# One kernel in two stages becomes one stream of 128-token units, with the attention output kept on chip

## The chip, the cores and the metric

The kernel runs on one core of one Trainium2 chip. A core has a matrix engine (PE, whose weight loads are shown as PEld), a vector engine (DVE), an activation engine (ACT), a general engine (POOL), and a queue engine (SP) that issues transfers. Fast memory (SBUF) has 128 partitions; PE writes into accumulation banks (PSUM). The metric is the device time of one execution in microseconds (us). The time of a kernel is the median of several runs.

## The reference

The inputs q, k and v have 8 batches, 8 heads, 576 tokens and 64 elements per head. Each token attends to the tokens at most 32 places away:

```
scores = (q @ k^T) / 8          where |i - j| <= 32, else masked
attn   = exp(scores) / row sum  (a maximum is subtracted first, which cancels)
a      = attn @ v
x      = a, heads side by side: 4608 tokens x 512
h      = x @ w_in               512 x 2048
g      = h * sigmoid(1.702 h)
out    = g @ w_out              2048 x 512, float32
```

All inputs are float32. The kernels compute the products in bfloat16.

## The kernel before, in words

It runs in two stages, one behind the other, with the attention output in device memory between them (`x_bridge`).

**Attention** goes over 8 batches. For q and k it loads five blocks of 128 tokens (the last has 64), 256 KB each in runs of 256 bytes (L81), casts each to bfloat16 on DVE (L83), transposes four pairs of heads on PE (L86) and copies the result out of PSUM on DVE (L87). Then it goes over nine blocks of 64 queries. For each it loads its window of 128 keys of v again (L94, nine loads of 256 KB a batch), casts it on ACT (L96), multiplies eight heads' scores (L104, 64x64), takes the exponential in two halves into float32 (L107), casts these to bfloat16 (L109), cuts the band with two selects on POOL (L110, L113), multiplies with v and a column of ones (L120), and divides by the sum (L125, L127). The 64 rows of x go to device memory (L128).

**The two layers (MLP)** begin with the weights: 4 loads of w_in (L147) and 16 of w_out (L152), each with a DVE cast (L148, L153). Then nine tiles of 512 tokens follow. Each loads x transposed, by four transposing transfers (L159). In 16 steps `ff`, four matmuls of 512 columns make one 128-row piece of h (L165), ACT makes g from it (L168), and four matmuls add it into four banks of output (L170). Four copies (L174) and four stores (L175) close the tile; `o_sb` has two buffers, and the four output banks have one each.

A planner orders the instructions of each engine. Transfers all go through SP's queue, in order; the MLP's pools open when those of attention have closed.

## Time and profile before

| what | value |
|---|---|
| runs shown | 595.07, 594.59, 594.83 us; median 594.83 |
| the profiled execution | its own time is given as its span, 594.3 us; the runs' median is 0.5 us above it |
| busy, share of the span | PE 64%, PEld 31%, DVE 29%, ACT 36%, POOL 17% |
| transfers | 65.51 MB in 183333 packets, 171520 of them under 512 bytes |
| device memory | read 46.14 MB, written 14.16 MB |

A share of busy time is a mean over stages that differ. PE's matmuls are pipelined: their shown durations overlap, so a row's whole length over its count is the pace, and the mean of one is its latency. "Idle before" says how long an engine waited ahead of a group and what ended that wait. The granted clock is the share of PE's full clock of 2.4 GHz.

### The profile page before, as it was taken

Reading aid. Unit: us, or ns where it says so; the run is one execution under the profiler, and the core shown is the slowest. Engines: PE = TensorE matmul, PEld = TensorE weight load, DVE = VectorE, ACT = ScalarE, POOL = GpSimd, SP = SyncE. Lnnn points to the kernel's source line nnn. Section 1 sums busy time; section 2 is a strip of 40 time slices with the busy share of each in tenths; the row PEclk is TensorE's granted clock in tenths of the full one; section 3 lists DMA queues with packets and bytes.
Section 4 is the critical chain, followed back from the end, with each engine's and each line's share of the span. In section 5 each row is a group of like instructions: output and inputs, shape, how many; then the busy total and the mean of one; then the engine's idle time right before and its main releaser. Section 6 shows DMA issues by size and latency. Waiting matters only on the chain.

```text
span 594.3 us, 7458 instructions
## 1 busy us (share of the span) xinstructions
PE 379.6 (64%) x2624; PEld 186.8 (31%) x2624; DVE 170.9 (29%) x504; ACT 213.6 (36%) x434; POOL 102.0 (17%) x222
## 2 busy tenths in 40 slices
PE   2525335252533525253069798997989898989994
PEld 1423223141322414232024343333334333333431
DVE  2545445454543535454222200000010101010101
ACT  1725436172543617246013233232323232323331
POOL 0613416071341606235000000000000000000000
PEclk9999999999999999999999999899989999999999
DMA  7576685857668576765865302102030303030101
GB/s 166 122 167 147 156 183 129 184 126 156 144 156 185 128 168 140 152 145 121 296 149 174 111 16 67 41 19 88 10 98 1 106 1 106 1 103 4 72 0 72
DMA packets 183333, 65.51 MB, mean 110 GB/s; under 512 B 171520, under 2 KB 176128, under 8 KB 182784
## 3 DMA queue, kind: packets, MB, share of 16 engines
q1 hardware_dynamic: 183296, 65.03, 44.4%
q8 instruction: 21, 0.34, 0.3%
q14 instruction: 16, 0.13, 0.1%
HBM read 46.14 MB, written 14.16 MB: 101 GB/s over the span
## 4 chain that ended last, share of the span: by engine, by line
PE 39%; SPq 5%; DMA 5%; issue 2%; DVE 2%; ACT 0%; DVEq 0%; ACTq 0%
PE ops L170 20%; PE h_ps L165 19%; SPq L159 5%; DMA out_dram<-o_sb 3%; DVE o_sb L174 1%; DMA wtmp<-in_moe_w_in_dram 1%; DMA xT<-x_bridge 1%; DVE w_in_sb L148 0%; ACT g_sb L168 0%; DVEq L174 0%; SPq L152 0%; SPq L175 0%; DVEq L148 0%; ACTq L168 0%
## 5 line engine op out<-in xcount | busy, mean ns | idle before, releaser
L168 ACT ACTIVATE g_sb<-h_ps 128x512 bf16<-128x512 f32 x144 | 85.9, 597 | 218.1 <-PE h_ps L165 218.1
L165 PE MATMUL h_ps<-xT,w_in_sb 128*128 128x512 bf16 x576 | 146.4, 391 | 22.1 <-DVE w_out_sb L153 18.9
L170 PE MATMUL ops<-w_out_sb,g_sb 128*128 128x512 bf16 x576 | 144.1, 384 | 21.9 <-DVE o_sb L174 20.8
L86 PE MATMUL tps<-ident,qktmp 128*128 128x128 bf16 (+1 forms) x320 | 45.1, 293 | 86.2 <-DVE qktmp L83 82.0
L174 DVE COPY o_sb<-ops 128x512 f32<-128x512 f32 x36 | 23.8, 689 | 237.9 <-PE ops L170 198.8
L120 PE MATMUL oa<-v_aug,pbf 128*64 128x65 bf16 x576 | 47.4, 245 | 63.2 <-ACT v_aug L96 53.1
L165 PEld LDWEIGHTS <-w_in_sb 128*128 128x128 bf16 x576 | 57.5, 100 | 95.3 <-issue 31.6
L96 ACT CAST v_aug<-v_f 128x512 bf16<-128x512 f32 x72 | 44.6, 620 | 107.1 <-DMA v_f<-in_v_dram 104.2
L170 PEld LDWEIGHTS <-g_sb 128*128 128x128 bf16 x576 | 46.3, 98 | 108.0 <-ACT g_sb L168 46.8
L110 POOL TENSOR_SCALAR_AFFINE_SELECT pbf<-pbf 128x512 bf16<-128x512 bf16 x72 | 47.8, 663 | 157.8 <-ACT pbf L109 157.8
L107 ACT ACTIVATE p<-sc 128x256 f32<-128x256 f32 x144 | 49.1, 389 | 35.6 <-PE sc L104 35.2
L120 PEld LDWEIGHTS <-pbf 128*64 128x64 bf16 x576 | 38.3, 153 | 72.8 <-issue 42.1
L86 PEld LDWEIGHTS <-qktmp 128*128 128x128 bf16 (+1 forms) x320 | 26.0, 128 | 100.0 <-DVE qktmp L83 97.9
L127 DVE TENSOR_TENSOR ob<-oa,inv 64x256 bf16<-64x256 f32 x144 | 56.1, 410 | 1.2 <-DVE inv L125 0.5
L113 POOL TENSOR_SCALAR_AFFINE_SELECT pbf<-pbf 128x512 bf16<-128x512 bf16 x72 | 49.7, 690 | 2.8
L109 ACT CAST pbf<-p 128x512 bf16<-128x512 f32 x72 | 44.8, 622 | 9.5 <-PE oa L120 7.6
L83 DVE CAST qktmp<-qktmpf 128x512 bf16<-128x512 f32 (+1 forms) x80 | 37.5, 469 | 34.3 <-DMA qktmpf<-in_q_dram 22.4
L125 DVE RECIPROCAL inv<-oa 64x4 f32<-64x4 f32 x144 | 19.2, 162 | 70.5 <-PE oa L120 70.2
L104 PE MATMUL sc<-qT,kT 64*128 64x64 bf16 x576 | 28.8, 236 | 14.6 <-DVE kT L87 8.1
L104 PEld LDWEIGHTS <-kT 64*128 64x128 bf16 x576 | 18.8, 120 | 24.2 <-DVE kT L87 16.6
L87 DVE COPY qT<-tps 128x512 bf16<-128x512 bf16 (+1 forms) x40 | 15.9, 397 | 24.2 <-PE tps L86 24.2
L87 DVE COPY kT<-tps 128x512 bf16<-128x512 bf16 (+1 forms) x40 | 15.8, 395 | 15.4 <-PE tps L86 15.4
(11 smaller groups left out, 23.2 us busy)
## 6 DMA issues: line engine op xcount, KB each, us to landing
v_f<-in_v_dram SPq DMA_DIRECT2D x72, 256.0 KB, 3.5
out_dram<-o_sb SPq DMA_DIRECT2D x36, 256.0 KB, 2.1
qktmpf<-in_q_dram SPq DMA_DIRECT2D x32, 256.0 KB, 3.5
qktmpf<-in_k_dram SPq DMA_DIRECT2D x32, 256.0 KB, 3.3
x_bridge<-ob SPq DMA_DIRECT2D x72, 64.0 KB, 2.1
wtmp<-in_moe_w_in_dram SPq DMA_DIRECT2D x4, 1024.0 KB, 5.3
wtmp<-in_moe_w_out_dram SPq DMA_DIRECT2D x16, 256.0 KB, 2.6
qktmpf<-in_q_dram SPq DMA_DIRECT2D x8, 128.0 KB, 3.0
```

The source lines that it names most:

```text
L86: nc.tensor.transpose(tps[:, hp, :si], tmp[:si, hp * 2:hp * 2 + 2, :], ident[:si, :si])
L96: nc.scalar.copy(vt[:, :, :D], vtf)
L104: nc.tensor.matmul(scl[eo][:, hq, :], kT[hr:hr + D, hp, ks0:ks0 + 128], qT[hr:hr + D, hp, q0:q0 + SQ], start=(hq == 0), stop=(hq == 3))
L107: nc.scalar.activation(pbig[:, eo, :, :], scl[eo], AF.Exp, scale=scale)
L109: nc.scalar.copy(pbf, pbig)
L110: nc.gpsimd.affine_select(out=pbf, in_=pbf, compare_op=ALU.is_ge, fill=0.0, base=off + 32, pattern=[[0, 2], [0, 4], [-1, SQ]], channel_mul ...
L113: nc.gpsimd.affine_select(out=pbf, in_=pbf, compare_op=ALU.is_ge, fill=0.0, base=-off + 32, pattern=[[0, 2], [0, 4], [1, SQ]], channel_mul ...
L120: nc.tensor.matmul(oal[eo][:, hq, :], pbf[:, eo, hq, :], vt[:, h, :], start=(hq == 0), stop=(hq == 3))
L127: nc.vector.tensor_mul(obig[:, :, eo, :], oal[eo][:, :, :D], inv_b)
L165: nc.tensor.matmul(h_ps, w_in_sb[:, kr, ff * 128:(ff + 1) * 128], xT[:, kr, :], start=(kr == 0), stop=(kr == NK - 1))
L168: nc.scalar.activation(g_sb, h_ps, AF.Gelu_apprx_sigmoid)
L170: nc.tensor.matmul(o_ps[ts], g_sb[:, ts * 128:(ts + 1) * 128], w_out_sb[:, ff, :], start=(ff == 0), stop=(ff == NFF - 1))
```

## The change

The two stages become one program of 36 units of 128 tokens (two query blocks each) and nine tiles of 512 tokens (four units), written out by hand in the order that each engine keeps (`manual_schedule`). `head` runs the first tile apart; from unit 8 on `run` puts into one step: scores of unit n, the second layer of tile t-2, transposes of a coming batch, values of unit n, and the first layer of tile t-1.

x is transposed on PE from SBUF (`x_T`) and never leaves the chip. q and k are loaded with six neighbouring tokens per partition (96 partitions, runs of 1536 bytes). v is loaded once, into key blocks of 128 that begin at even windows (`ve`); the odd windows (`vo`) are copied from there by transfers between partitions on POOL's queue. The exponential is written in bfloat16, and the band is cut by a DVE product with a mask that is made once. The second layer runs over the whole g of a tile, one 128-row block of output at a time.

```diff
+    def bank(self, kind, shape, dtype, name):
+        bufs = {"h": 2, "o": 1, "sc0": 1, "sc1": 1, "pv0": 1, "pv1": 1, "tp": 1}[kind]
+        return self.ps.tile(shape, dtype, name=name, tag=kind, bufs=bufs)
+
...
+        self.w_out_sb = cst.tile([128, self.NFF, self.DM], BF16, name="w_out_sb")
+        self.qT = [cst.tile([128, 4, self.S], BF16, name=f"qT{i}") for i in range(2)]
+        self.kT = [cst.tile([128, 4, self.S + 64], BF16, name=f"kT{i}") for i in range(2)]
+        self.ve = [cst.tile([128, 5, self.H, 66], BF16, name=f"ve{i}") for i in range(2)]
...
+    def setup_mask(self):
+        m = self.mask
+        self.nc.gpsimd.memset(m, 1.0)
+        for i in range(5):
+            blk = m[:, i * SQ:(i + 1) * SQ]
+            _select(self.nc, blk, 0, -1, 1)
+            _select(self.nc, blk, 64, 1, -1)
+            if i == 2:
+                _select(self.nc, blk, 95, 0, -1)
+            if i == 3:
+                _select(self.nc, blk, -32, 0, 1)
+
...
+    def load_w_in(self, c):
+        w = self.DFF // 4
+        raw = self.raw.tile([128, self.NK, w], F32, name="w_raw", tag="w_raw", bufs=2)
+        self.nc.sync.dma_start(raw, self.w_in[:, c * w:(c + 1) * w].rearrange("(k p) f -> p k f", p=128))
+        self.raws["wi", c] = raw
+
+    def cast_w_in(self, c, eng):
+        w = self.DFF // 4
+        raw = self.raws.pop(("wi", c))
+        for kr in range(self.NK):
+            self.cast(eng, self.w_in_sb[:, kr, c * w:(c + 1) * w], raw[:, kr, :])
+
+    def load_w_out(self, c):
+        raw = self.raw.tile([128, 4, self.DM], F32, name="w_raw", tag="w_raw", bufs=2)
+        self.nc.sync.dma_start(raw, self.w_out[512 * c:512 * (c + 1), :].rearrange("(k p) f -> p k f", p=128))
+        self.raws["wo", c] = raw
+
+    def cast_w_out(self, c, eng):
+        raw = self.raws.pop(("wo", c))
+        for fr in range(4):
+            self.cast(eng, self.w_out_sb[:, 4 * c + fr, :], raw[:, fr, :])
+
+    def load_qk(self, b, parts=1):
+        for name, src in (("k", self.k), ("q", self.q)):
+            self.raws[name, b] = self.raw.tile([PT, self.H, JT * self.D], F32, name=name + "_raw", tag=name + "_raw")
+        n = self.H // parts
+        for i in range(parts):
+            for name, src in (("k", self.k), ("q", self.q)):
+                self.nc.sync.dma_start(self.raws[name, b][:, i * n:(i + 1) * n, :],
+                                       src[b, i * n:(i + 1) * n].rearrange("h (p j) d -> p h (j d)", j=JT))
+
+    def cast_qk(self, b, which, hp, eng):
+        keep = self.ks if which == "k" else self.qs
+        if hp == 0:
+            keep[b] = self.work.tile([PT, 4, JT, 2, self.D], BF16, name=which + "s", tag=which + "s")
+        raw = self.raws[which, b][:, 2 * hp:2 * hp + 2, :].rearrange("p h (j d) -> p j h d", d=self.D)
+        self.cast(eng, keep[b][:, hp], raw)
+
+    def load_v(self, b):
+        raw = self.raw.tile([128, 5, self.H, self.D], F32, name="v_raw", tag="v_raw")
+        for m in range(5):
+            lo, hi, p = self.v_rows(m)
+            self.nc.sync.dma_start(raw[p, m, :, :], self.v[b, :, lo:hi, :].rearrange("h s d -> s h d"))
+        self.raws["v", b] = raw
+
+    def v_rows(self, m):
+        lo, hi = max(0, 128 * m - 32), min(self.S, 128 * m + 96)
+        p0 = lo - (128 * m - 32)
+        return lo, hi, slice(p0, p0 + hi - lo)
+
+    def cast_v(self, b, m, eng):
+        p = self.v_rows(m)[2]
+        for s in ([slice(32, 64), slice(64, 128)] if p.start else [p]):
+            self.cast(eng, self.ve[b % 2][s, m, :, :self.D], self.raws["v", b][s, m, :, :])
+
+    def shift_v(self, b, lo, hi):
+        ve, vo = self.ve[b % 2], self.vo[b % 2]
+        self.nc.gpsimd.dma_start(vo[0:64, lo:hi, :, :], ve[64:128, lo:hi, :, :])
+        self.nc.gpsimd.dma_start(vo[64:128, lo:hi, :, :], ve[0:64, lo + 1:hi + 1, :, :])
+
+    def heads_T(self, b, which, hp, kind="tp", eng=None):
+        nc = self.nc
+        src = (self.ks if which == "k" else self.qs)[b]
+        tp = self.bank(kind, [128, JT, PT], BF16, "tp")
+        for j in range(JT):
+            nc.tensor.transpose(tp[:, j, :], src[:, hp, j],
+                                self.ident[:PT, :PT])
+        if which == "k":
+            dst = self.kT[b % 2][:, hp, 32:32 + self.S]
+        else:
+            dst = self.qT[b % 2][:, hp, :]
+        self.cast(eng or nc.vector, dst.rearrange("r (p j) -> r p j", j=JT), tp.rearrange("r j p -> r p j"))
+
+    def blocks(self, u):
+        return [divmod(2 * u + i, NB) for i in range(2)]
+
+    def scores(self, u):
+        nc = self.nc
+        sc = [self.bank(f"sc{eo}", [128, 4, 2, SQ], F32, f"sc{eo}") for eo in range(2)]
+        n = 0
+        for blk, (b, j) in enumerate(self.blocks(u)):
+            for hp in range(4):
+                for eo in range(2):
+                    r = slice(eo * 64, eo * 64 + 64)
+                    nc.tensor.matmul(sc[eo][:, hp, blk, :], self.kT[b % 2][r, hp, 64 * j:64 * j + 128],
+                                     self.qT[b % 2][r, hp, 64 * j:64 * j + 64],
+                                     start=(n == 0), stop=(n == 7))
+                n += 1
+        p = self.work.tile([128, 2, 4, 2, SQ], BF16, name="p", tag="p", bufs=5)
+        for eo in range(2):
+            nc.scalar.activation(p[:, eo], sc[eo], AF.Exp, scale=self.scale)
+        self.p[u] = p
+
+    def band(self, u):
+        nc = self.nc
+        p = self.p[u]
+        (b0, j0), (b1, j1) = self.blocks(u)
+        first = {8: 2, 7: 1}.get(j0, 3 if j0 == 0 else 0)
+        msk = self.mask[:, first * SQ:(first + 2) * SQ].rearrange("p (o w) -> p o w", o=1)
+        for eo in range(2):
+            pv = p[:, eo].rearrange("p h b s -> p h (b s)")
+            nc.vector.tensor_mul(pv, pv, msk.to_broadcast([128, 4, 2 * SQ]))
+
+    def values(self, u):
+        nc, D = self.nc, self.D
+        p = self.p.pop(u)
+        x = self.work.tile([128, self.H, D], BF16, name="x", tag="x", bufs=3)
+        rec = self.work.tile([128, self.H, 1], F32, name="rec", tag="rec", bufs=3)
+        acc = [self.bank(f"pv{i}", [128, 4, D + 1], F32, f"pv{i}") for i in range(2)]
+        for half in range(2):
+            for hh in range(4):
+                h = 4 * half + hh
+                for blk, (b, j) in enumerate(self.blocks(u)):
+                    vt = (self.vo if j % 2 else self.ve)[b % 2]
+                    nc.tensor.matmul(acc[half][blk * 64:blk * 64 + 64, hh, :], p[:, h % 2, h // 2, blk, :],
+                                     vt[:, j // 2, h, :D + 1], start=(hh == 0), stop=(hh == 3))
+        for half in range(2):
+            hs = slice(4 * half, 4 * half + 4)
+            nc.vector.reciprocal(rec[:, hs, :], acc[half][:, :, D:D + 1])
+            nc.vector.tensor_mul(x[:, hs, :], acc[half][:, :, :D], rec[:, hs, :].to_broadcast([128, 4, D]))
+        self.x[u] = x
+
+    def x_T(self, u):
+        nc = self.nc
+        t, s = divmod(u, 4)
+        if s == 0:
+            self.xT[t] = self.work.tile([128, self.NK, 512], BF16, name="xT", tag="xT")
+        x = self.x.pop(u)
+        tp = self.bank("tp", [128, 4, 128], BF16, "tp")
+        for c in range(4):
+            nc.tensor.transpose(tp[:, c, :], x[:, 2 * c:2 * c + 2, :], self.ident)
+        nc.vector.tensor_copy(self.xT[t][:, :, s * 128:(s + 1) * 128], tp)
+
+    def layer1(self, t, ff):
+        nc = self.nc
+        if ff == 0:
+            self.g[t] = self.work.tile([128, self.NFF, 512], BF16, name="g", tag="g")
+        hps = self.bank("h", [128, 512], F32, "h_ps")
+        for kr in range(self.NK):
+            nc.tensor.matmul(hps, self.w_in_sb[:, kr, ff * 128:(ff + 1) * 128], self.xT[t][:, kr, :],
+                             start=(kr == 0), stop=(kr == self.NK - 1))
+        nc.scalar.activation(self.g[t][:, ff, :], hps, AF.Gelu_apprx_sigmoid)
+
+    def layer2(self, t, s, quarter, kind="o"):
+        nc = self.nc
+        if quarter == 0:
+            self.o_ps[t, s] = self.bank(kind, [128, self.DM], F32, "o_ps")
+        o_ps = self.o_ps[t, s]
+        for ff in range(4 * quarter, 4 * quarter + 4):
+            nc.tensor.matmul(o_ps, self.g[t][:, ff, s * 128:(s + 1) * 128], self.w_out_sb[:, ff, :],
+                             start=(ff == 0), stop=(ff == self.NFF - 1))
+        if quarter == 3:
+            o_sb = self.work.tile([128, self.DM], F32, name="o_sb", tag="o_sb", bufs=4)
+            nc.vector.tensor_copy(o_sb, o_ps)
+            row = t * 512 + s * 128
+            nc.sync.dma_start(self.out[row:row + 128, :], o_sb)
+
+    def head(self):
+
+        nc, dve, act = self.nc, self.nc.vector, self.nc.scalar
+        self.load_qk(0, parts=4)
+        self.setup()
+        self.load_v(0)
+        for c in range(2):
+            self.load_w_in(c)
+        kinds = ("h", "tp", "h", "o")
+        for hp in range(4):
+            self.cast_qk(0, "k", hp, dve)
+            self.cast_qk(0, "q", hp, act)
+            self.heads_T(0, "k", hp, kinds[(2 * hp) % 4], dve)
+            self.heads_T(0, "q", hp, kinds[(2 * hp + 1) % 4], act)
+        self.setup_mask()
+        for u in range(4):
+            self.scores(u)
+            self.cast_v(0, u, dve)
+            if u > 0:
+                self.shift_v(0, u - 1, u)
+            self.band(u)
+        self.cast_v(0, 4, dve)
+        self.shift_v(0, 3, 4)
+        self.load_w_in(2)
+        self.load_w_in(3)
+        self.load_qk(1, parts=4)
+        self.cast_w_in(0, act)
+        for u in range(4):
+            self.values(u)
+            self.x_T(u)
+        for c in range(2):
+            self.load_w_out(c)
+        for ff in range(16):
+            if ff in (0, 4, 8):
+                self.cast_w_in(ff // 4 + 1, dve)
+            self.layer1(0, ff)
+            if ff >= 9 and ff % 2:
+                hp = (ff - 9) // 2
+                self.cast_qk(1, "k", hp, dve)
+                self.cast_qk(1, "q", hp, dve)
+                self.heads_T(1, "k", hp)
+                self.heads_T(1, "q", hp, "o")
+        self.load_w_out(2)
+        self.load_w_out(3)
+        self.load_v(1)
+        self.load_qk(2)
+        kinds = ("o", "h", "h", "pv1")
+        for c in range(4):
+            self.cast_w_out(c, dve)
+            self.scores(4 + c)
+            self.band(4 + c)
+            for s in range(4):
+                self.layer2(0, s, c, kinds[s])
+        for m in range(5):
+            self.cast_v(1, m, dve)
+            if m > 0:
+                self.shift_v(1, m - 1, m)
+        self.load_v(2)
+
+    def run(self):
+        nc = self.nc
+        self.head()
+        first_u = [(NB * b) // 2 for b in range(self.B)]
+        last_u = [(NB * (b + 1) - 1) // 2 for b in range(self.B)]
+
+        def later(n):
+
+            t, s = divmod(n, 4)
+            a1, a2 = [], []
+            if 2 <= t < 2 + self.NU // 4 - 1:
+                ffs = range(4 * s, 4 * s + 4)
+                a1 = [lambda ff=ff: self.layer1(t - 1, ff) for ff in ffs]
+            if t >= 3:
+                kind = ("o", "h")[s % 2] if not a1 else "o"
+                a2 = [lambda i=i: self.layer2(t - 2, s, i, kind) for i in range(4)]
+            return a1, a2
+
+        for n in range(4, self.NU + 8):
+            a1, a2 = later(n)
+            tr = []
+            for b in range(2, self.B):
+                free = last_u[b - 2] + 1
+                if n in (free - 1, free):
+                    for hp in range(2 * (n - free + 1), 2 * (n - free + 2)):
+                        self.cast_qk(b, "k", hp, nc.vector)
+                        self.cast_qk(b, "q", hp, nc.vector)
+                if free <= n < free + 4:
+                    tr = [lambda b=b, w=w, hp=n - free: self.heads_T(b, w, hp) for w in "kq"]
+                    for m in ((0, 1, 2), (3, 4), (), ())[n - free]:
+                        self.cast_v(b, m, nc.gpsimd)
+                    if n == free + 2:
+                        self.shift_v(b, 0, 4)
+                if b + 1 < self.B and n == free + 1:
+                    self.load_qk(b + 1)
+                    self.load_v(b + 1)
+
+            def fill(a, n):
+                for _ in range(min(n, len(a))):
+                    a.pop(0)()
+
+            if 8 <= n < self.NU:
+                self.scores(n)
+            fill(a2, 1)
+            fill(tr, 1)
+            fill(a2, 1)
+            fill(tr, 1)
+            if 8 <= n < self.NU:
+                self.band(n)
+            fill(a2, 2)
+            if n < self.NU:
+                self.values(n)
+            fill(a1, 2)
+            if n < self.NU:
+                self.x_T(n)
+            fill(a1, 2)
 
...
+    kern = _Kernel(ctx, tc, q, k, v, moe_w_in, moe_w_out, out)
+    with tc.manual_schedule():
+        kern.run()
```

## Rows read from the trace of the kernel before

**Rows 1.** The page: busy tenths of PE and its granted clock in 40 slices.

```profile
PE   2525335252533525253069798997989898989994
...
PEclk9999999999999999999999999899989999999999
```

**Rows 2.** Busy us (x instructions) per engine in three stretches; clock, DMA share, GB/s.

```profile
0.00:280.90 280.90, 116.07 (x1472) 82.95 (x1472) 135.30 (x448) 126.36 (x289) 101.96 (x222) 1.00 0.68 152
280.90:298.90 18.00, 0.00 (x0) 0.00 (x0) 5.24 (x6) 1.28 (x1) 0.00 (x0) 1.00 0.74 263
298.90:594.30 295.40, 263.53 (x1152) 103.81 (x1152) 30.31 (x52) 85.95 (x144) 0.00 (x0) 0.98 0.21 61
```

**Rows 3.** Who waited for whom: us in total, times, longest us.

```profile
ACT v_aug L96 <- DMA v_f<-in_v_dram: 104.2, 32, 8.4
...
PE ops L170 <- DVE o_sb L174: 20.8, 7, 3.0
```

**Rows 4.** Chain that ended last, MLP: start us, us, what.

```profile
359.63 1.73 PE h_ps L165 x8
361.36 1.79 PE ops L170 x8
...
374.45 2.42 PE h_ps L165 x6
```

**Rows 5.** Timeline of attention, small matmuls: start us, us, engine, line, shapes, count [idle before].

```profile
119.05 0.61 PE L86 MATMUL tps<-ident,qktmp 128*128 128x128 bf16 x4 [0.54 <-DVE qktmp L83]
...
120.17 0.61 PE L104 MATMUL sc<-qT,kT 64*128 64x64 bf16 x16 [0.52 <-DVE kT L87]
...
127.94 0.65 PE L120 MATMUL oa<-v_aug,pbf 128*64 128x65 bf16 x8 [0.29 <-POOL pbf L113]
...
128.52 0.39 PE L86 MATMUL tps<-ident,qktmp 64*128 64x64 bf16 x4
```

**Rows 6.** Groups by line and shape: busy us, mean ns of one | idle before.

```profile
L168 ACT ACTIVATE g_sb<-h_ps 128x512 bf16<-128x512 f32 x144 | 85.9, 597 | 218.1 <-PE h_ps L165 218.1
...
L127 DVE TENSOR_TENSOR ob<-oa,inv 64x256 bf16<-64x256 f32 x144 | 56.1, 410 | 1.2 <-DVE inv L125 0.5
L113 POOL TENSOR_SCALAR_AFFINE_SELECT pbf<-pbf 128x512 bf16<-128x512 bf16 x72 | 49.7, 690 | 2.8
...
L174 DVE COPY o_sb<-ops 128x512 f32<-128x512 f32 x36 | 23.8, 689 | 237.9 <-PE ops L170 198.8 <-DMA out_dram<-o_sb 37.5 <-PE h_ps L165 1.6
...
L125 DVE RECIPROCAL inv<-oa 64x4 f32<-64x4 f32 x144 | 19.2, 162 | 70.5 <-PE oa L120 70.2
...
L87 DVE COPY kT<-tps 128x512 bf16<-128x512 bf16 x32 | 13.6, 425 | 15.4 <-PE tps L86 15.4
...
L153 DVE CAST w_out_sb<-wtmp 128x512 bf16<-128x512 f32 x16 | 6.8, 427 | 24.0 <-DMA wtmp<-in_moe_w_out_dram 24.0
...
L148 DVE CAST w_in_sb<-wtmp 128x2048 bf16<-128x2048 f32 x4 | 4.9, 1227 | 12.8 <-issue 7.1 <-DMA wtmp<-in_moe_w_in_dram 5.6
...
L168 ACT ACT_TABLE_LOAD x1 | 1.3, 1283 | 1.7 <-DVE ob L127 1.7
```

**Rows 7.** The page, DMA issues: KB each, median us from issue to landing.

```profile
out_dram<-o_sb SPq DMA_DIRECT2D x36, 256.0 KB, 2.1
```

**Rows 8.** Slices of the span (columns as in Rows 2), for DMA rates.

```profile
0.00:14.90 14.90, 3.36 (x24) 2.17 (x24) 4.37 (x12) 2.71 (x4) 0.92 (x10) 1.00 0.80 166
...
282.30:297.10 14.80, 0.00 (x0) 0.00 (x0) 3.68 (x3) 0.06 (x1) 0.00 (x0) 1.00 0.80 296
...
579.40:594.30 14.90, 7.36 (x33) 2.71 (x32) 2.62 (x4) 2.39 (x4) 0.00 (x0) 0.91 0.19 71
```

**Rows 9.** Timeline, the end (columns as in Rows 5).

```profile
586.47 1.04 PE L170 MATMUL ops<-w_out_sb,g_sb 128*128 128x512 bf16 x4 [0.75 <-ACT g_sb L168]
...
589.80 1.33 DVE L174 COPY o_sb<-ops 128x512 f32<-128x512 f32 x2 [1.61 <-DMA out_dram<-o_sb]
```

**Rows 10.** The stretch behind one tile boundary (columns as in Rows 2).

```profile
372.40:376.70 4.30, 4.27 (x12) 1.60 (x12) 0.64 (x1) 0.60 (x1) 0.00 (x0) 0.60 0.34 124
```

More of the change, by code (lines that the diff above doesn't have):

```diff
@@ L20 @@
 ALU = mybir.AluOpType
-def _make_band_mask(nc, out_ap, offset, valid=1.0, mask=0.0):
-    p, f = out_ap.shape
-    nc.gpsimd.memset(out_ap, valid)
-    nc.gpsimd.affine_select(
-        out=out_ap, in_=out_ap, compare_op=ALU.is_ge, fill=mask,
-        base=offset + 32, pattern=[[-1, f]], channel_multiplier=1)
-    nc.gpsimd.affine_select(
-        out=out_ap, in_=out_ap, compare_op=ALU.is_ge, fill=mask,
-        base=-offset + 32, pattern=[[1, f]], channel_multiplier=-1)
+SQ = 64
+NB = 9
+JT = 6
@@ L131 @@
-    NK = DM // 128
-    NFF = DFF // 128
-    TOK_TILE = 512
-    NM = NTOK // TOK_TILE
-    TS = TOK_TILE // 128
-    with (
-        tc.tile_pool(name="w", bufs=1) as w_pool,
-        tc.tile_pool(name="xw", bufs=2) as xw_pool,
-        tc.tile_pool(name="gw", bufs=3) as gw_pool,
-        tc.tile_pool(name="ow", bufs=2) as ow_pool,
-        tc.tile_pool(name="psm", bufs=1, space=bass.MemoryType.PSUM) as psm_pool,
-    ):
-        w_in_sb = w_pool.tile([128, NK, DFF], BF16, name="w_in_sb")
-        for kr in range(NK):
-            tmp = xw_pool.tile([128, DFF], F32, name="wtmp", tag="wtmp")
-            nc.sync.dma_start(tmp, moe_w_in[kr * 128:(kr + 1) * 128, :])
-            nc.vector.tensor_copy(w_in_sb[:, kr, :], tmp)
-        w_out_sb = w_pool.tile([128, NFF, DM], BF16, name="w_out_sb")
-        for fr in range(NFF):
-            tmp = xw_pool.tile([128, DM], F32, name="wtmp", tag="wtmp")
-            nc.sync.dma_start(tmp, moe_w_out[fr * 128:(fr + 1) * 128, :])
-            nc.vector.tensor_copy(w_out_sb[:, fr, :], tmp)
-        for mi in range(NM):
-            tok0 = mi * TOK_TILE
-            xT = xw_pool.tile([128, NK, TOK_TILE], BF16, name="xT", tag="xT")
-            for kr in range(NK):
-                nc.sync.dma_start(xT[:, kr, :], x_dram.ap()[tok0:tok0 + TOK_TILE, kr * 128:(kr + 1) * 128], transpose=True)
-            o_ps = [psm_pool.tile([128, DM], F32, name=f"ops{ts}", tag=f"ops{ts}", bufs=1) for ts in range(TS)]
-            for ff in range(NFF):
-                h_ps = psm_pool.tile([128, TOK_TILE], F32, name="h_ps", tag="h_ps", bufs=3)
-                for kr in range(NK):
-                    nc.tensor.matmul(h_ps, w_in_sb[:, kr, ff * 128:(ff + 1) * 128], xT[:, kr, :],
-                                     start=(kr == 0), stop=(kr == NK - 1))
-                g_sb = gw_pool.tile([128, TOK_TILE], BF16, name="g_sb")
-                nc.scalar.activation(g_sb, h_ps, AF.Gelu_apprx_sigmoid)
-                for ts in range(TS):
-                    nc.tensor.matmul(o_ps[ts], g_sb[:, ts * 128:(ts + 1) * 128], w_out_sb[:, ff, :],
-                                     start=(ff == 0), stop=(ff == NFF - 1))
-            for ts in range(TS):
-                o_sb = ow_pool.tile([128, DM], F32, name="o_sb")
-                nc.vector.tensor_copy(o_sb, o_ps[ts])
-                nc.sync.dma_start(out[tok0 + ts * 128:tok0 + (ts + 1) * 128, :], o_sb)
@@ L179 @@
+    assert tuple(q.shape) == (8, 8, 576, 64)
+    kern = _Kernel(ctx, tc, q, k, v, moe_w_in, moe_w_out, out)
+    with tc.manual_schedule():
+        kern.run()
 _INS = ['q', 'k', 'v', 'moe_w_in', 'moe_w_out']
```

117 lines of the change are left out of this document (40 added, 77 removed).

## The prediction

> **What bounds the kernel now.** I read the slices first. PE is busy 2 to 5 tenths in the first 19 and 7 to 9 in the last 20, so the kernel has two stages with different limits [rows 1]. The stretches put numbers on this: attention takes 280.9 us and PE shows 116.1 us busy in it; then 18.0 us pass without a matmul while weights arrive; the MLP takes 295.4 us [rows 2]. Next I read the waits. In attention ACT waits 104.2 us for loads of v, and DMA engines are busy 68% of that stretch: nothing is full, but every block walks through load, cast, transpose, exponential, select and product. In the MLP, seven waits of PE for a copy of the output cost 20.8 us [rows 3]. Last, the chain: inside a tile it is PE alone, eight matmuls of 512 columns per 1.73 us, 0.216 us each, and 1.79 where they stand behind Gelu [rows 4]. The 1152 of them need 1152 x 0.216 = 249 us, so 46 of the MLP's 295.4 us are waits at boundaries and the start.
>
> So whatever lays attention beside the big matmuls leaves PE's sum as the floor. I work that out first, then what each stretch of the new order adds.
>
> **PE's sum.** Pace of the small matmuls, from group length less one latency: scores (0.61 - 0.24)/15 = 0.025 us, products with v (0.65 - 0.25)/7 = 0.058, transposes of 128 columns (0.61 - 0.31)/3 = 0.10, of 64 columns (0.39 - 0.24)/3 = 0.05 [rows 5] (the latency is that of one matmul of the group). The change has 576 scores and 576 products as before, 144 transposes of x (0.10 each) and 384 of q and k with 96 columns (between 0.05 and 0.10; I take 0.09, nearest to the 128-wide row). Per unit: scores 16 x 0.025 = 0.40, products 16 x 0.058 = 0.93, x 0.40. In all 14 + 33 + 14 + 35 = 97 us. With 249 that is 346 us for PE.
>
> **Units 12 to 35, the full stream.** PE: 32 big matmuls 6.91 + 0.40 + 0.93 + 0.40 = 8.64 us. Hand-offs between engines: five groups per unit begin behind a semaphore. The row behind Gelu pays 0.03 us per wait (1.79 against 1.73 for two) [rows 4]; a group that must also load its first weights late pays more. I take 0.35 per unit, bounds 0.15 and 0.6. So 9.0 us, and 24 x 9.0 = 216. In 17 of these units (one of batch 3, four each of batches 4 to 7) 12 transposes and their waits add 1.15: 19.6. Together 236 us.
>
> Is PE really last there? Four checks.
> - ACT: two exponentials of 128x512 and four Gelu, each 0.60 by the Gelu row, make 3.6 us. The two functions lie in different tables: the row has a load of 1.28 us ahead of the first Gelu [rows 6]. In a stream that alternates, this load comes twice per unit: 6.2 us, under 9.0.
> - The chain from the last Gelu to the products: Gelu 0.7, load 1.28, two exponentials 1.2, the band's second half 0.5, hand-off 0.1 = 3.8 us after the scores begin. PE's cover for it is the scores and 16 second-layer matmuls, 0.40 + 3.46 = 3.86. It just fits. If that cover is gone the unit stalls by what is missing.
> - DVE, fullest unit: four casts of 768 elements (0.43 + 256 x 0.52 ns = 0.56 each, the slope from the casts of 512 and 2048), two copies of 576 out of PSUM (0.46 by the bf16 copy, 0.76 by the float32 one; I take 0.74, since these read with a stride), two band products (0.43 by the bf16 copy of the same size, 0.69 by the slope of float32 work; I take 0.5), reciprocals 2 x 0.16, divisions 2 x 0.41, x copy 0.43, output copy 0.69 = 7.0 us [rows 6]. Below PE's 10.2 in such a unit, at the upper prices too (7.4).
> - POOL: three casts of v in one unit, no row; a pass over the same 128x512 took POOL 0.69 [rows 6], twice that would still be 4 us, and their readers come a unit or more later. Stores on SP's queue stand behind loads of the next batch, which wait for a cast of the unit before; `o_sb` has four buffers, so 3 units of slack cover this.
>
> **Units 8 to 11.** There is no second layer yet, so only scores and transposes (1.6 us) cover the chain, and four casts on DVE push the band to 4.3. Then products 0.93, two first-layer steps 1.73, x 0.40, two more 1.73: 9.2 us each, 37 us. The bounds are PE's work alone, 6.5, and 10.
>
> **Units 36 to 43 and the end.** Four tiles' quarters of both layers, 4 x 6.95, four of the second alone, 4 x 3.46 = 41.7. Behind the last matmul: copy 0.69, store 2.1 [rows 7], and the 1.1 us that pass today between that point and the end (last copies end at 591.1, plus 2.1, span 594.3) [rows 9]; 4.0 with a hand-off. Today 6.7 us lie there, since the last two copies wait for a buffer. Sum 46.
>
> **The head, until unit 8 starts.** This is the uncertain term. What it moves: q and k of three batches 7.1 MB, v of two 2.4, weights 8.4. Rates at full engines: 256-byte runs 166/0.80 = 207 GB/s; 8 KB runs of w_in 296/0.80 = 370; 2 KB stores 71/0.19 = 374 [rows 8]. The 1536-byte runs have no row: from 207 to 370. I take 300 for all but v (190), as nothing keeps the queue always full. The walk, in us:
> - q, k of batch 0 by 10, v by 16, two quarters of w_in by 23. Four rounds of cast, transposes, copy (2.7 each, half of them under the loads): 14.5. Scores and exponentials, one bank each: 4 x 2.0, done at 22.5. Products, division, x, strictly in turn: 4 x 2.9 from 21, done at 33.
> - First layer of tile 0, 16 x 0.87 = 14, from 33. The last quarter of w_in waits for a buffer whose cast stands on DVE behind unit 3's x: issued at 35. Behind it on SP's queue stand q and k of batch 1: 38.5 to 46.5, landed at 48.5; their casts and transposes lie in PE's order inside this layer. It ends at 51.5 rather than 47.
> - w_out: two quarters by 53.5, the third waits for the cast of the first (54), the last for the second's (57.3): landed 63, cast 65. Second layer of tile 0: its last quarter ends at 68.5.
> - Behind these, v of batch 1 (61 to 67) and q, k of batch 2 (67 to 75, landed 77). In unit 4 four casts of batch 2 precede the division in DVE's order, so DVE stands until 78.7; unit 4 ends at 80.5.
> - Units 5 to 7 have no MLP at all. Two sets of transposes and x share one bank: three rounds of 0.55 + 0.74 + 0.1, products 0.93, division 0.2: 5.3 us each. Unit 8 begins at 97.
> PE's own work in it is 55 us. Bounds: 75 (transfers at 370 and the casts hidden) and 115 (1536-byte runs at 207 add 11, the rest PE at half clock behind long idles: after 3 us idle the granted clock was 0.60 over 4.3 us, one half and full mixed [rows 10]).
>
> **Sum.** 97 + 37 + 236 + 46 = 416 us of span; the median stood 0.5 us above the span before: 416.
>
> **Rivals.**
> - A, a shorter head. For it: weights ran at 296 GB/s with DMA engines 80% busy [rows 8]. Against: the waits for two weight buffers are in the order. If the head takes 75 us: 394. Chance 0.15.
> - B, the switch of tables holds ACT longer than its row. No row of before shows what follows a load directly: one precedes a wait for data, so ACT's own recovery can't be seen. If a switch costs twice its row, the chain is 5.1 against 3.86: 1.25 us in 11 units without other cover, 0.3 in 17, and Gelu pressing on the h banks about 0.3 in 28: 14 + 5 + 8 = 27 us, 443. Chance 0.22.
> - C, the stream doesn't overlap: a late link stops PE in every unit, and attention's chain stands beside the MLP instead of under it. Chain 3.8 + 0.93 + 1.3 + 0.4 = 6.4 us x 28 against the 1.7 counted: +130, about 545. Against: the big matmuls of a unit depend on nothing made in that unit. Chance 0.06, 0.01 of it no change.
> - D, slower than before. The clock. Idles of 3 us per unit would hold PE at half clock, where big matmuls take 2.42/6 = 0.403 us [rows 4]: 1152 x 0.403 = 464, small ones 97 x 1.6 = 155, head's waits 45: 664. It decides once the chain is 3 us longer than its cover in every unit. Against: attention ran at granted clock 1.00 with PE busy 41% [rows 2]. Chance 0.03.
>
> For B the Trainium skill has a rule, in ScalarE: Activation LUTs, "What ACT_TABLE_LOAD costs": every switch to another set costs about 2.66 us, 1.28 of load and some 1.38 of drain, and functions should be batched by set. The trace agrees with the load alone, 1283 ns [rows 6]; by the page's 2.66 the sum would be an estimated 445, by the row 416. It speaks against alternating Exp and Gelu as this change does.
>
> **How the numbers follow.** The forecast's own case, 402 to 432, has 0.54; A 0.15, B 0.22, C 0.06, D 0.03. The range 388 to 450 takes in the forecast, B and most of A, about 0.83. Faster by over 0.2% (about what a measurement of this kernel can tell from no change): 0.54 + 0.15 + 0.22 + 0.05 = 0.96; same 0.01; slower 0.03.
>
> **What would show it.** Right: from unit 12 PE nearly gapless, 9 to 10.2 us per unit, 32 big matmuls at 0.216; two table loads per unit with ACT idle otherwise; a first stretch of some 97 us with PE about half busy, waiting for casts of weights and of batch 2. Wrong: PE waiting for the band in each unit (B), a granted clock near 0.5 (D), or a head whose waits are not transfers. The forecast falls if the full units take over 10.5 us or the head under 80.

## The result, and the profile after

The changed kernel takes 398.09 us (median of 4 runs, 396.51 to 399.29) against 594.71 us for the kernel before in the same measurement: 0.6688 of its time, 95% interval 0.6654 to 0.6722. The forecast was 416 us. The profiled execution's span is 397.1 us (398.76 us its own time). A control in a later measurement gave 398.41 (0.6707, 0.6687 to 0.6728); that is the base of the differences below.

The page of the kernel after, the slices that answer to [rows 1] and the slices of the DMA engines, shows one stage where there were two: PE starts irregularly for a quarter of the span, at half clock in its last part, and is then full to the end.

```profile
PE   3548999025377799998999999899989989999996
...
PEclk9999999555588899999999999999999999999999
DMA  8985989999959302593289024953000100011012
```

The windows of the kernel after, in the prediction's stages (columns as in [rows 2]): the head in four stretches, units 8 to 11, the full stream, the rest.

```profile
0.00:23.40 23.40, 8.59 (x115) 5.90 (x115) 12.52 (x32) 13.05 (x21) 8.23 (x27) 1.00 1.04 247
23.40:33.90 10.50, 7.08 (x83) 3.85 (x85) 7.81 (x26) 1.84 (x3) 0.00 (x0) 1.00 0.46 139
33.90:68.70 34.80, 33.69 (x235) 15.38 (x237) 22.53 (x50) 15.18 (x25) 0.00 (x0) 1.00 0.95 259
68.70:101.10 32.40, 9.24 (x117) 6.03 (x116) 17.54 (x40) 0.00 (x0) 9.65 (x16) 0.54 1.10 243
101.10:140.80 39.70, 27.27 (x257) 14.23 (x262) 19.39 (x45) 22.28 (x30) 7.21 (x12) 0.77 0.69 134
140.80:350.20 209.40, 200.97 (x1796) 99.83 (x1830) 110.19 (x257) 143.40 (x191) 16.43 (x28) 1.00 0.39 92
350.20:397.10 46.90, 42.98 (x196) 19.35 (x198) 5.95 (x9) 11.14 (x19) 0.00 (x0) 0.98 0.12 46
```

| stage | predicted | measured |
|---|---|---|
| until the scores of unit 8 | 97 | 101.1 |
| units 8 to 11 | 37 | 39.7 |
| units 12 to 35 (140.8 to about 351.7) | 236 | 211 |
| the rest | 46 | 45.4 |

Three stages agree within 5 us and are together 6 us longer than forecast; the third is 25 us shorter, which leaves the miss of 19. The timeline of two of its units (start us, us, engine, line, count) shows where. From scores to scores the first, without transposes of q and k, takes 157.53 - 149.47 = 8.06 us (predicted 9.0), the second, with them, 166.25 - 157.53 = 8.72 (10.15).

```profile
149.47 0.41 PE L183 MATMUL sc<-qT,kT 64*128 64x64 bf16 x16
150.03 3.40 PE L249 MATMUL o_ps<-w_out_sb,g 128*128 128x512 bf16 x15 [0.16 <-PE sc L183]
153.37 0.45 PE L213 MATMUL pv<-ve,p 128*64 128x65 bf16 x16
155.48 0.39 PE L229 MATMUL tp<-ident,x 128*128 128x128 bf16 x4
157.53 0.41 PE L183 MATMUL sc<-qT,kT 64*128 64x64 bf16 x16
158.74 0.42 PE L164 MATMUL tp<-ident,ks 96*128 96x96 bf16 x6
...
166.25 0.41 PE L183 MATMUL sc<-qT,kT 64*128 64x64 bf16 x16
```

The waits of PE in the full stream come to less than 8 us in 209 (us in total, times, longest); for the band they are 0.4 us:

```profile
PE h_ps L239 <- ACT g L241: 4.7, 5, 0.9
PE o_ps L249 <- issue: 1.1, 7, 0.2
...
PE pv L213 <- DVE p L200: 0.4, 2, 0.2
```

In the 140.8 us before it, PE waits for DVE, and behind DVE for transfers (waits of that stretch, then three rows of the chain; the 81.31 us row of the timeline shows DVE standing 5.96 us for q of batch 2):

```profile
PE tp L229 <- DVE x L218: 17.8, 12, 12.6
PE tp L164 <- DVE kT L96: 10.4, 7, 3.4
```

```profile
41.25 13.66 DMA w_raw<-in_moe_w_out_dram
...
66.66 14.63 DMA q_raw<-in_q_dram
...
87.54 16.00 DMA q_raw<-in_q_dram
```

```profile
81.31 0.56 DVE L96 CAST qs<-q_raw 96x768 bf16<-96x768 f32 x1 [5.96 <-DMA q_raw<-in_q_dram]
...
83.41 0.40 PE L229 MATMUL tp<-ident,x 128*128 128x128 bf16 x2 [12.60 <-DVE x L218]
```

### The profile page after: what moved, and what is told of

It is laid out like the page before. It is cut to its first block, busy times and chain, and to the rows that moved or that the text cites. A ratio compares the mean times of both kernels' runs of the same rounds, so it can differ in the third digit from the quotient of the medians.

```text
span 397.1 us, 6783 instructions
## 1 busy us (share of the span) xinstructions
PE 329.8 (83%) x2786; PEld 164.6 (41%) x2832; DVE 195.9 (49%) x458; ACT 206.9 (52%) x286; POOL 41.5 (10%) x83
## 4 chain that ended last, share of the span: by engine, by line
PE 67%; DMA 16%; DVE 8%; ACT 3%; SPq 3%; issue 2%; ACTq 0%; DVEq 0%
PE h_ps L239 28%; PE o_ps L249 27%; DMA q_raw<-in_q_dram 11%; PE tp L164 4%; DMA w_raw<-in_moe_w_out_dram 3%; PE pv L213 3%; PE sc L183 2%; SPq L140 2%; PE tp L229 2%; DVE p L200 2%; ACT L241 2%; DMA vo<-ve 2%; DVE x L218 1%; DVE qT L96 1%; DVE qs L96 1%
## 5 line engine op out<-in xcount | busy, mean ns | idle before, releaser
L241 ACT ACTIVATE g<-h_ps 128x512 bf16<-128x512 f32 x144 | 85.4, 597 | 102.1 <-PE h_ps L239 102.0
L249 PE MATMUL o_ps<-w_out_sb,g 128*128 128x512 bf16 x552 | 131.7, 379 | 2.5 <-issue 1.1
L249 PEld LDWEIGHTS <-g 128*128 128x128 bf16 x576 | 52.1, 98 | 55.7 <-issue 1.3
L189 ACT ACTIVATE p<-sc 128x512 bf16<-128x512 f32 x72 | 39.1, 595 | 47.5 <-PE sc L183 47.2
L96 DVE COPY kT<-tp 128x576 bf16<-128x576 bf16 x32 | 24.2, 756 | 53.3 <-PE tp L164 53.0
L253 DVE COPY o_sb<-o_ps 128x512 f32<-128x512 f32 x36 | 24.8, 690 | 45.7 <-PE o_ps L249 45.7
L241 ACT ACT_TABLE_LOAD x29 | 37.2, 1283 | 15.3 <-PE h_ps L239 14.9
L200 DVE TENSOR_TENSOR p<-p,mask 128x512 bf16<-128x512 bf16 x72 | 30.2, 442 | 30.3 <-ACT p L189 29.6
L96 POOL CAST ve<-v_raw 128x512 bf16<-128x512 f32 (+3 forms) x36 | 23.2, 647 | 168.5 <-DMA v_raw<-in_v_dram 113.5
L189 ACT ACT_TABLE_LOAD x28 | 35.9, 1283 | 0.5
L218 DVE TENSOR_TENSOR x<-pv,rec 128x256 bf16<-128x256 f32 x72 | 30.5, 424 | 2.5
L96 DVE COPY qT<-tp 128x576 bf16<-128x576 bf16 x28 | 21.1, 755 | 13.0 <-PE tp L164 13.0
L229 PEld LDWEIGHTS <-x 128*128 128x128 bf16 x144 | 11.2, 104 | 29.1 <-DVE x L218 21.5
```

What stands on the lines that cost most here:

```text
L96: (eng.copy if eng is self.nc.scalar else eng.tensor_copy)(out, in_)
L189: nc.scalar.activation(p[:, eo], sc[eo], AF.Exp, scale=self.scale)
L200: nc.vector.tensor_mul(pv, pv, msk.to_broadcast([128, 4, 2 * SQ]))
L218: nc.vector.tensor_mul(x[:, hs, :], acc[half][:, :, :D], rec[:, hs, :].to_broadcast([128, 4, D]))
L229: nc.tensor.transpose(tp[:, c, :], x[:, 2 * c:2 * c + 2, :], self.ident)
L241: nc.scalar.activation(self.g[t][:, ff, :], hps, AF.Gelu_apprx_sigmoid)
```

## The experiments

Differences are against 398.4 us unless another base is named. Each ratio stands against the kernel before in the same measurement.

**The control.** The changed kernel again.

> The changed kernel once more, on the chip of the runs beside it. Both theories: 398 us, give or take 1.5.

398.41 us (397.33 to 399.4).

**The products, block by block.** Is the short product group due to neighbours that write different halves of the output?

```diff
-            for hh in range(4):
-                h = 4 * half + hh
-                for blk, (b, j) in enumerate(self.blocks(u)):
+            for blk, (b, j) in enumerate(self.blocks(u)):
+                for hh in range(4):
+                    h = 4 * half + hh
```

> The 16 products with v of a unit are issued query block by query block, not alternating between the two halves of the output's partitions. Theory: alternation lets two products run side by side. At half clock 16 took 0.65 us, as long as 8 in the kernel before; so alone they should pace at 0.03 us at full clock, 16 in 0.64 instead of 0.45. From unit 8 on PE sets the time, 28 to 32 units pay 0.2: +6 to +8 us, up to +16 if the weight loads also come to light. Rival: the faster pace is the clock's alone; then the change is within 1 us.

399.48 us (0.6717, 0.6692 to 0.6742): no change, a miss. The edit did not take away what it was meant to. Its timeline shows products that read `vo` (the one block) and `ve` (the other) still starting in turn, though the program as written now has four of one block and then four of the other:

```profile
161.09 0.22 PE L213 MATMUL pv<-vo,p 128*64 128x65 bf16 x1
161.11 0.22 PE L213 MATMUL pv<-ve,p 128*64 128x65 bf16 x1
161.15 0.20 PE L213 MATMUL pv<-vo,p 128*64 128x65 bf16 x1
161.16 0.20 PE L213 MATMUL pv<-ve,p 128*64 128x65 bf16 x1
```

So this run says nothing for or against; the pace had to be measured by itself.

**Halves apart.** Behind the last tile, four batches of 64 products into banks that are free there: batches 1 and 3 write one half of the 128 output rows, batches 2 and 4 the two in turn.

```diff
+        for kind, halves in (("pv0", 1), ("pv1", 2), ("pv0", 1), ("pv1", 2)):
+            junk = self.bank(kind, [128, 4, 65], F32, "junk")
+            for i in range(64):
+                lo = 64 * (i % halves)
+                nc.tensor.matmul(junk[lo:lo + 64, (i // halves) % 4, :], ...)
```

> Behind the last unit four groups of 64 more products of the same size (64x64 weights columns, 65 columns) run on a warm PE, into a bank that nobody reads: all into one half of the output's partitions, then alternating between halves, twice. Theory: products into different halves run side by side, so the first kind paces at 0.027 to 0.030 us, the second at half of it, 0.014 to 0.017. Rival: pace is the clock's alone, both kinds are equal. The kernel gets 4 to 7 us longer, which says nothing.

404.13 us, one run. Windows of half a microsecond inside the batches (us, PE busy and how many products, clock, DMA share, GB/s):

```profile
395.50:396.00 0.50, 0.50 (x22) 1.00 0.00 0
397.50:398.00 0.50, 0.50 (x44) 1.00 0.24 74
```

Twice as many run when the halves alternate. A window counts every product that overlaps it, so the time for its count is 0.5 us and one latency of 0.195, 0.695 us: 0.695/22 = 0.032 us each in one half, 0.695/44 = 0.016 alternating. All four batches by these are 128 x 0.032 + 128 x 0.016 = 6.1 us; their row is 6.27 us long, 6.1 without one latency. The second pair of batches shows the same counts, 22 and 44. Two output halves do run side by side.

**One table.** Exp is replaced by the function of the first layer, so that no table is switched between units; the attention weights are then not those of the reference.

```diff
-            nc.scalar.activation(p[:, eo], sc[eo], AF.Exp, scale=self.scale)
+            nc.scalar.activation(p[:, eo], sc[eo], AF.Gelu_apprx_sigmoid, scale=self.scale)
```

> Exp is replaced by the Gelu function, so no tables are switched (the attention weights are then not those of the reference). Theory: a switch costs its 1.28 us row on ACT and is hidden under PE but for five units where the load itself waits for the first layer's matmuls (4.7 us of PE's waits in all) and some of units 8 to 11: -4 to -8 us. Rival: the switch costs twice its row and presses on every unit: -15 us or more.

392.25 us (0.6606, 0.6587 to 0.6626): 6.2 less. The 56 switches between the two functions, behind the first, cost 6 us together. The timeline of the kernel after shows why: ACT does them in time that it has, one behind the other without a gap (Gelu ended at 319.22, Exp starts 0.02 us behind the load). Only in 5 units does the load itself wait for the first layer's matmuls, and then PE stands 0.94 us for Gelu:

```profile
318.62 0.60 ACT L241 ACTIVATE g<-h_ps 128x512 bf16<-128x512 f32 x1 [0.27 <-PE h_ps L239]
319.23 1.28 ACT L189 ACT_TABLE_LOAD   x1
320.53 1.08 ACT L189 ACTIVATE p<-sc 128x512 bf16<-128x512 f32 x2
...
323.91 1.28 ACT L241 ACT_TABLE_LOAD   x1 [2.29 <-PE h_ps L239]
...
325.85 1.89 PE L239 MATMUL h_ps<-xT,w_in_sb 128*128 128x512 bf16 x8 [0.94 <-ACT g L241]
```

With one table the waits of 4.7 us are gone; the other 1.5 us are about the width of these intervals, and their place was not sought.

**The second quarter of w_in cast on ACT.** Is the head bound by transfers from end to end? Then an earlier buffer shifts all that follows.

```diff
+        self.cast_w_in(1, act)
...
-            if ff in (0, 4, 8):
+            if ff in (4, 8):
```

> The second quarter of w_in is cast on ACT right behind the first, no longer on DVE behind unit 3's x; so the last quarter of w_in and all loads behind it are issued some 6 us earlier. Theory: the head until unit 8 is bound by transfers, whose one gap lies from 25 to 34 us (DMA share 0.46): -4 to -7 us. Rival: the head is bound by the order of PE and DVE, and the loads wait elsewhere: within 1 us.

397.66 us (0.6694, 0.6675 to 0.6713): 0.7 less, within the intervals. The edit did what it was meant to, and the gain was lost on the way: the loads of batch 1 are issued at 28.9 us instead of 33.9, those of v of batch 1 at 56.1 instead of 56.8. The theory falls. The chain of this kernel has, behind 33.9 us, the first layer of tile 0 at PE's pace and the casts of batch 1 in its order, where the theory had transfers; only the stretch from w_out's third quarter on is set by transfers.

**Tile 1's layers early.** In units 4 to 7 there is no work of the two layers (9.24 us of PE in the 32.4 us up to 101.1). Here tile 1's first layer runs before unit 8, and its second layer in units 8 to 11, where the stream had none.

```diff
+        one = [lambda ff=ff: self.layer1(1, ff) for ff in range(16)]
...
+            if n < 12:
+                a1, a2 = [], [lambda i=i, s=n - 8: self.layer2(1, s, i) for i in range(4)]
+            elif n < 16:
+                a1, a2 = a1[2:], a1[:2]
```

> Units 4 to 7 finish before anything of batch 2 is asked for; the first layer of tile 1 runs between the transposes of batch 2; units 8 to 11 then carry tile 1's second layer and units 12 to 15 only tile 2's first layer. Theory: PE's waits of 23 us from 69 to 101 us and some 12 us in units 8 to 11 stand behind loads of batch 2 that nothing else needs, and big matmuls can fill them: -18 to -27 us. Rival: the transfers bound everything up to unit 12, so that the work that was moved is waited for later: -5 us at most.

384.48 us (0.6465, 0.6437 to 0.6492): 13.9 less, of an expected 18 to 27. The mechanism holds and the size was too large: from 68.7 to 101.1 us PE is now busy 20.59 us instead of 9.24, not full, since one wait of 5.9 us for shifted v of batch 1 and others for DVE stay.

**PE kept warm.** Matmuls whose result nothing reads are put into units 4 to 11, so that the clock doesn't fall.

```diff
+        def warm(n, k):
+            if n < 12:
+                junk = self.bank("o", [128, 512], F32, "junk")
+                for i in range(k):
+                    nc.tensor.matmul(junk, self.w_out_sb[:, i, 0:128], self.w_in_sb[:, 0, 0:512], ...)
```

> In units 4 to 11 PE gets groups of 4 to 6 matmuls of 512 columns into a bank that nobody reads, where it waits. Theory: the half clock from 70 to 112 us and the mixed one to 140 us (granted 0.50, then 0.83 to 0.89) make the small groups there last 0.61 and 0.64 instead of 0.41 and 0.42 us and some big ones twice as long: -3 to -7 us. Rival: the waits there are for transfers and DVE, so that the clock costs nothing, and the added groups lie in the way: 0 to +4 us.

395.2 us (0.6644, 0.6617 to 0.667): 3.2 less, with the time of the added matmuls in it. The 16 scores of unit 8 in the kernel after, with the window around them (granted 0.50, the 1.2 GHz level, after 32 us in which PE was busy 29%), and the same scores in this kernel:

```profile
101.11 0.61 PE L183 MATMUL sc<-qT,kT 64*128 64x64 bf16 x16
```

```profile
98.00:101.80 3.80, 2.63 (x44) 1.80 (x44) 2.51 (x8) 0.05 (x1) 0.00 (x0) 0.50 1.12 225
```

```profile
100.76 0.41 PE L183 MATMUL sc<-qT,kT 64*128 64x64 bf16 x16
```

Half clock makes 0.61 of 0.41. By the starts of the scores the gain lies in units 8 to 11, which take 36.8 us instead of 39.7; unit 8 starts 0.4 us earlier (1.3 against the control's profile), so the head loses little by it. In the kernel before the same 16 scores took 0.61 [rows 5], though its window there says 1.00:

```profile
120.10:120.80 0.70, 0.61 (x16) 0.45 (x16) 0.02 (x1) 0.47 (x2) 0.70 (x3) 1.00 0.51 118
```

The kernel after has the same at its own start. Six transposes of 96 columns take 0.66 us at 4.66, where the window from 4 to 14 us says 1.00 with PE busy 55%; 0.64 at 91.73, where 84 to 99 us say 0.50; and 0.42 at 158.74 in the full stream:

```profile
4.66 0.66 PE L164 MATMUL tp<-ident,ks 96*128 96x96 bf16 x6 [4.66 <-DVE ks L96]
91.73 0.64 PE L164 MATMUL tp<-ident,ks 96*128 96x96 bf16 x6 [0.52 <-DVE xT L230]
```

**Both: w_in on ACT and tile 1 early.**

> The early second quarter of w_in on ACT and the early first layer of tile 1 together. Theory: both gains add, as one shifts the loads and the other fills the wait behind them: -22 to -34 us against the changed kernel, 364 to 376 us. Rival: transfers bound both: no more than the better of the two alone.

385.62 us (0.6477, 0.6451 to 0.6504): no better than tile 1 early alone, so the gains do not add. That transfers are the reason, as the rival has it, was not shown.

**Runs of 256 bytes.** q and k are loaded with the tokens of a partition 96 apart, so that the copies out of PSUM read and write without a stride.

```diff
-                                       src[b, i * n:(i + 1) * n].rearrange("h (p j) d -> p h (j d)", j=JT))
+                                       src[b, i * n:(i + 1) * n].rearrange("h (j p) d -> p h j d", j=JT))
```

> q and k are loaded with token j*96+p in place j of partition p, so in runs of 256 bytes instead of 1536, and the copies behind the transposes read and write in straight order. Theory: the head is bound by transfers, 7.1 MB of q and k go at some 200 instead of 270 GB/s, +9 us, and up to +20 if the queue is also slower to issue; the copies get shorter (from 0.76 to some 0.46 us), which PE-bound units don't notice. Rival: run length is nothing and the copies matter: -2 to -6 us.

404.59 us (0.6799, 0.6765 to 0.6833): 6.2 more, the sum of two opposite effects. By the starts of the scores, unit 8 comes 6.4 us later and itself takes 16.5 us instead of 13.1, 9.8 more in all, near the 9 expected for the transfers. The copies fall from 756 to 456 ns, and against the expectation the full stream feels it: from the scores of unit 12 to those of unit 35 it takes 199.6 us instead of 203.0, a unit with transposes 8.58 instead of 8.72. There the transposes of q start 1.13 us behind those of k instead of 1.27; both go through one bank (`tp`), which the copy of k must empty first. The first window shows 205 GB/s, all loads together, where the kernel after has 247, at a DMA share that rose from 1.04 to 1.20:

```profile
0.00:23.40 23.40, 8.58 (x113) 5.89 (x113) 10.15 (x29) 10.68 (x16) 6.59 (x24) 1.00 1.20 205
```

**The stream not interleaved.** Same work in the same units, but four units of attention first and then the two layers of a tile.

```diff
+            if 12 <= n < self.NU:
+                late += a2 + a1
+                if n % 4 == 0:
+                    self.scores(n)
+                fill(tr, 2)
+                if n % 4 < 3:
+                    self.scores(n + 1)
+                self.band(n)
+                self.values(n)
+                self.x_T(n)
+                if n % 4 == 3:
+                    fill(late, len(late))
+                continue
```

> From unit 12 on, four units of attention run one behind the other (scores one unit ahead), then the 32 groups of both layers of a tile; nothing else is changed. Theory: the gain of the stream is that big matmuls cover the chain exponential, band, products, division; without it a unit's attention stands alone with some 5 us (DVE with casts and copies up to 6.5) in front of 27.6 us of big matmuls per tile: 47 instead of 35 us per tile, six tiles: +70 us, 470, bounds +45 and +90. Rival: the saving is in the leaner attention itself, and the tables are switched 4 times less often: within 10 us of 398.

501.93 us (0.8457, 0.842 to 0.8495): 103.5 more, over the upper bound. PE's waits over the span are now those of attention's chain, and the window shows what the expectation left out, a granted clock of 0.76 where the stream had 1.00:

```profile
PE tp L229 <- DVE x L218: 35.6, 63, 12.9
PE tp L164 <- DVE kT L96: 31.7, 24, 3.2
PE pv L213 <- DVE p L200: 19.4, 21, 2.2
```

```profile
200.00:260.00 60.00, 44.46 (x360) 23.28 (x360) 23.86 (x55) 17.55 (x28) 4.63 (x8) 0.76 0.39 86
```

Between 140 and 440 us the waits of PE come to some 68 us, where the stream had less than 8. The clock and the rest of the 103.5 were not separated. So without the fine order of the instructions 103.5 of the 195.7 us that the control gains are lost.

**v of batch 1 early.** On top of both edits, v of batch 1 is loaded before the second half of w_out and cast on POOL.

```diff
+        self.load_v(1)
...
+        for m in range(5):
+            self.cast_v(1, m, nc.gpsimd)
+            if m > 0:
+                self.shift_v(1, m - 1, m)
```

> The early first layer of tile 1 and early second quarter of w_in, and besides v of batch 1 is loaded ahead of the second half of w_out and cast on POOL, so that units 4 to 7 find it. Theory: PE's 8 us of waits from 69 to 81 us for v of batch 1 (casts, the copies between partitions) go, and nothing else of that stretch is late by more than 2 us: -5 to -9 us against the kernel without it, 376 to 381 us. Rival: the stretch is bound by q and k of batch 2, which now come later: within 1 us of 385.

380.44 us (0.6394, 0.6365 to 0.6424; 6 runs, 377.05 to 381.67), about 5 less than both edits alone, at the lower end of what was expected. It is the fastest of all that were run. PE is busy 27.16 us from 68.7 to 101.1, where both edits alone had 21.53 and the kernel after 9.24. Between 33 and 141 us the wait of 5.8 us for shifted v is gone, and four waits for casts of w_out have come, 4.1 us, the longest 2.6: more than the 2 us expected.

**x through device memory again.** On the kernel with w_in on ACT (397.66), x is stored and read back with transposing transfers, as before the change; the rest stays.

```diff
-        for c in range(4):
-            nc.tensor.transpose(tp[:, c, :], x[:, 2 * c:2 * c + 2, :], self.ident)
-        nc.vector.tensor_copy(self.xT[t][:, :, s * 128:(s + 1) * 128], tp)
+        nc.sync.dma_start(self.x_dram.ap()[u * 128:(u + 1) * 128, :], ...)
+        if s == 3:
+            for c in range(4):
+                nc.sync.dma_start(self.xT[t][:, c, :], ..., transpose=True)
```

> x goes through device memory again: each unit stores its 128 rows, and behind the fourth unit of a tile four transposing transfers bring the tile back (all on SP's queue); PE no longer transposes x and DVE no longer copies it. The rest is the kernel with the early second quarter of w_in on ACT (397.7 us). Theory: the way through memory takes the division, a store of 2.1, four issues of 1.26 and 2.7 us to land, some 11 us, and the order has 7.7 us of other matmuls to cover it: 3 us at each of eight tiles, and more in the head, where the stores stand behind loads on SP's queue; PE is spared 36 x 0.22 = 8 us: +25 us, bounds +5 and +60. Rival: the stream is deep enough to hide it, keeping x on chip is worth nothing and PE's 8 us come back: -8 to +3 us.

459.42 us (0.7721, 0.7672 to 0.7771): 61.8 more, just over the upper bound. The waits of PE, and one boundary in the timeline:

```profile
PE h_ps L240 <- DMA xT<-x_bridge: 58.0, 23, 19.9
```

```profile
195.95 14.48 SPq L141 DMA_DIRECT2D v_raw<-in_v_dram  x5
210.53 0.76 SPq L256 DMA_DIRECT2D out_dram<-o_sb  x1
211.39 0.38 SPq L228 DMA_DIRECT2D x_bridge<-x  x1
214.84 5.93 SPq L231 DMA_TRANSPOSE xT<-x_bridge  x4
...
217.40 0.58 PE L240 MATMUL h_ps<-xT,w_in_sb 128*128 128x512 bf16 x1 [7.49 <-DMA xT<-x_bridge]
```

x stands in SP's queue behind five loads of v and a store, waits 3.1 us for its own landing, and the four transposing transfers take 5.93 us to issue. By the starts of the scores the 62 us lie so: 12 before unit 8 (a first wait of 19.9 us in tile 0), 16 in units 8 to 11, 34 in the 24 full units. The waits named are 58 us; the granted clock, 0.89 to 0.94 from 140 to 380 us, accounts for some of the rest, and how much was not separated.

## Why the prediction was right, and where it was off

- **What bounds it.** Right. 1152 big matmuls keep 0.216 us (8 in 1.73 in the chain), and from unit 12 PE is busy 200.97 of 209.4 us.
- **Units 12 to 35.** The step that failed in size, by 25 us: "Pace of the small matmuls". By its own formula, group length less one latency (0.20 for scores, 0.21 for products, 0.24 and 0.22 for transposes), the stream's rows give scores (0.41 - 0.20)/15 = 0.014 us (0.025), products 0.24/15 = 0.016 (0.058), transposes of x 0.15/3 = 0.05 (0.10), of 96 columns 0.20/5 = 0.04 (0.09). Per unit that is 0.22 + 0.26 + 0.20 = 0.68 instead of 1.73. Hand-offs are what is left: 8.06 - 6.91 - 0.68 = 0.47 (0.35). The 12 transposes with their waits add 0.66 (1.15). So 24 x 8.06 + 17 x 0.66 + 5 waits of 0.94 for Gelu = 193.4 + 11.2 + 4.7 = 209.3, of some 211 measured. The paces alone are worth more than the 25: 24 x 1.05 = 25 and 17 x 12 x 0.05 = 10 us. Larger hand-offs (2.9), waits around the transposes (some 2) and the waits for Gelu, which had no term (4.7), gave back near 10. So the forecast of 416 came as near as it did by errors that offset each other, those 10 us and the 6 of the other stages.
- **Why the paces were wrong.** [rows 5] were taken as full clock because [rows 2] grant attention 1.00. Their durations are those of half clock: 0.61 us for 16 scores where the kernel after has 0.61 at a granted 0.50 and 0.41 at 1.00, and keeping PE warm turned the one into the other. For the kernel before this is read from equal durations; no run kept its PE warm. Of the products' 16 x 0.042 = 0.67 us per unit, 16 x (0.058 - 0.032) = 0.42 is the clock; 16 x 0.016 = 0.26 is the two halves side by side, which [rows 5] could not show.
- **The four checks.** Right. ACT's two loads per unit are there (29 and 28 loads of 1283 ns), and hidden but for the five waits of 0.94 us. The chain under its cover fits with 0.4 us of waits for the band in the whole stretch. Casts took 562 ns (0.56), strided copies 756 (0.74, near the upper bound), band products 442 (0.5, near the lower bound), POOL's casts 647.
- **Units 8 to 11.** 39.7 against 37, and not evenly. Unit 8 takes 13.06 us (101.11 to 114.17): in the chain its casts stand behind q of batch 3, which lands at 103.5, a wait that had no term. The other three take 7.74, 9.42 and 9.42 (9.2), their chain on DVE's copies and the band, as worked out; seven first-layer matmuls take 3.19 us in unit 10 and 1.67 in unit 9, so the clock (0.77 over the stretch) is in the longer two.
- **The end.** 45.4 against 46; the last copy begins at 393.43 and the span ends 3.7 us later (4.0).
- **The head.** 101.1 against 97. The transfers end later than walked (q of batch 2 at 81.3, not 77, with 247 and 259 GB/s in two loaded stretches where 300 was taken for all but v), so DVE stands until 82.8 instead of 78.7. From there to unit 8 it is 18.3 us, as worked out; that this fits has some luck in it, as PE works there at half clock and the walk used the paces of half clock without knowing it. That transfers set all of it is refuted: an earlier buffer gave 0.7 us. That its waits in part come from an order that can be changed is shown by 380.44 us.
- **Rival A**, a head of 75 us: no, as ordered. **Rival B**, a switch that costs twice its row: refuted by the trace (0.02 us behind the load) and by 6.2 us for all switches. The Trainium skill, in ScalarE: Activation LUTs, "What ACT_TABLE_LOAD costs", gives 1283 ns for the load, with which the 57 loads here agree (mean 1283), and a drain of about 1380 ns on top, which the rows shown don't have.
- **Rival C**, no overlap: no; the kernel with the coarse order took 103.5 us more, where C had 130 for a chain that stands beside the big matmuls in every unit. **Rival D**: the clock did not hold at a half in the stream. Its argument against, that attention ran at full clock while PE was 41% busy, does not hold: by its durations attention ran at half clock. With the coarse order the clock fell to 0.76, so D's mechanism shows where PE has gaps; the stream has hardly any.

## What to carry to other kernels

Before a pace is taken from a trace, compare the same form at two places: twice here, in attention before and in the head after, a granted clock of 1.00 stood beside durations that elsewhere belong to 0.50. When two stages are laid over each other, put the chain of the one between independent matmuls of the other in small pieces: here half of the gain went when that order was undone, and a third when x passed a transfer queue that other loads share. Once the stream is full, what is left lies in its start: move independent large work into it, which here gave 13.9 us.
